# ACT work that waits for DVE moved behind the next product's PSUM copy; transposes and routing spread over more slots

## The chip, the cores and the metric

The kernel runs on one core of a Trainium2 chip as one launch. A core has TensorE (PE) for matrix products, VectorE (DVE), ScalarE (ACT) and GpSimd (POOL) for elementwise work, SyncE (SP) that issues DMAs, an on-chip memory (SBUF) and the accumulators (PSUM) that PE writes. Each engine runs its own instructions strictly in the order in which the program emits them, and waits on semaphores for the others. The metric is device time in microseconds, from several runs of the same program; the profile shows one further execution.

## The reference

```
attn = softmax(q @ mean_pool8(k).T / sqrt(64)) @ mean_pool8(v)    # 4 batches, 8 heads, 576 rows, 64 wide
x = attn as [2304, 512]
P = exp(x @ w_gate - max);  8 times: P /= row sums; P /= column sums; P *= N / E     # routing, [2304, 8]
x = sum over 8 experts e of P[:, e] * (relu(x @ w1[e]) @ w2[e])   # 512 -> 1024 -> 512
g = x @ gate;  out = (g * sigmoid(g) * (x @ val)) @ out_w         # 512 -> 1536 -> 512, float64 weights
```

## The kernel before

Every product is made in three float32r passes: an operand is split into a high part (ACT copies it, `hh`, `ph`, `r`) and a low part (POOL or DVE subtracts the high part from the source, `hl`, `pl`), and PE multiplies high by high, high by low and low by high (lines 114 to 116 for the first layers, 1002 to 1004 for the second). A first phase computes attention and the first half of expert 0; there the eight routing rounds begin. The rest is 90 *quads* of expert work (three passes over 768 tokens, 30 quads each) and then 36 quads of the gated layer (18 steps of a gate quad and a value quad).

A quad computes a 2 by 2 block product by Winograd's seven products M1, M2, M5, M6, M7, M4, M3 in this order (`quad`). M1 goes to the PSUM tile `a`, M2 to `b`, M5 to `c`; M6, M7 and M4 accumulate on `a`, M3 on `c`. Partial sums are taken by ACT copies out of PSUM (line 948): `s1` after M1, `u2` after M6, `u3` after M7. So M6, which adds to `a` again, must wait for the copy `s1`, and M7 for `u2`. The four results 11, 22, 21, 12 go through a *sink*: DVE adds the partial sum (`csum`, line 1017), ACT takes the ReLU as high part (`hh`, 1019), DVE takes the low part (`hl`, 1020). 21 needs no sum and is read from PSUM directly. The second-layer tiles of the quad before (`ys`, six per quad, three PSUM buffers) are put in two at a time by `fill_y` after M6, M7 and M4; DVE adds each to its accumulator (`acc`, line 1107).

The order is written out by hand. After each product, and after each second-layer tile, `pump` runs what stands in `late` (DVE low parts, sigmoids), then the tasks that `next_weights` and the pass boundaries put at that product (splits of the next weights, `pair_hi` on ACT and `pair_lo` on POOL; splits of the token operands B11, B21, B22, T1 to T4; loads), then one step of the queue `side`. A quad has 13 such side slots when it has six tiles. `side` holds the routing (`route_rows`, one slot of nothing, `route_cols`), the transposes of finished tokens at the start of a pass (`transposed`: PE transposes into a `y` buffer, ACT copies it to `x2`, which has two buffers, SP stores it), and in passes 2 and 3 the conversion of the float64 weights (`convs`: DVE integer steps `c64t`, `c64s`, `c64u`, a POOL addition `c64w` and POOL sums).

In `quad` the sink is called before `pump`: ACT's `hh` of result 12, which waits for DVE's `csum`, is emitted after M3 and so stands in ACT's queue ahead of the next quad's `s1` copy, and `hl` is emitted right behind it.

Of the kernel before, what the change touches and what calls it, by code (L numbers as in the profile page):

```python
# [28 lines left out]
def fused_kernel(ctx: ExitStack, tc, q, k, v, w_gate, w1, w2, v_gate, v_val, v_out, out):  # L29
# [472 lines left out]
    with tc.manual_schedule():  # L502
# [146 lines left out]
        def load_pair(i):  # L649
            if i < len(quads):  # L650
                praw[i] = rawp.tile([P, KD, 2 * P], F32, tag="raw", name=f"praw{i}")
                if i < NE:
                    nc.sync.dma_start(out=praw[i], in_=quads[i].rearrange("(k p) f -> p k f", p=P))
                else:
                    n, g = quads[i]
                    nc.sync.dma_start(out=praw[i].rearrange("p k f -> p (k f)"), in_=w32_d[n][:, g])

        def row_of(i):
# [122 lines left out]
        for _ in range(ITERS):  # L781
            side.extend([route_rows, nothing, route_cols])

# [167 lines left out]
        def pump(tasks, m):  # L951
            later()
            for t in tasks.get(m, ()):
                t()
            if side:
                side.popleft()()

        def quad(i, ys, tasks, sink):

            def fill_y(n):  # L960
                for _ in range(n):
                    if ys:
                        ys.popleft()()
                        pump({}, None)

            per = -(-len(ys) // 3)
# [3 lines left out]
            pump(tasks, "M1")  # L970
# [6 lines left out]
            pump(tasks, "M5")  # L977
            product(a, i, "M6", False)
            u2 = part_sum(a, "u2")
            pump(tasks, "M6")  # L980
            fill_y(per)
            product(a, i, "M7", False)
            u3 = part_sum(a, "u3")
            sink("22", c, u3)
            pump(tasks, "M7")
            fill_y(per)
            product(a, i, "M4", False)
            sink("21", a, None)
            pump(tasks, "M4")
# [79 lines left out]
        for n in range(NS):  # L1069
# [3 lines left out]
            if l == 3:  # L1073
                merge(tasks, {m: [lambda t=t: scale_first(t), lambda t=t: scale_first(t + 1)]
                              for m, t in zip(("M1", "M2", "M5"), range(p * TT, (p + 1) * TT, 2))})
            if l == 4:
# [9 lines left out]
            if l == 1 and p > 0:  # L1086
                side.extendleft(reversed([lambda t=t: transposed(t) for t in range((p - 1) * TT, p * TT)]))
            if n == 3:
                assert not side
            if p > 0 and l not in (0, 1, SP1 - 1):  # L1090
                while len(side) < 13:
                    step = next(convs, None)
                    if step is None:
                        break
                    side.append(step)
            if n == 2:
                ahead["w"].close()
# [20 lines left out]
        gp = ctx.enter_context(tc.tile_pool(name="gp", bufs=1, **left))  # L1118

        nc.scalar.activation(out=small[:, 3:4], in_=ones[:, 0:1], func=AF.Sigmoid)  # L1120

        def gate_sink(gs):
            def sink(name, ps, t):
# [10 lines left out]

                late.append(sigmoid)
                gs[name] = g
# [21 lines left out]
        for m in range(NS2):  # L1158
# [65 lines left out]
```

## Time and profile before

| | us |
|---|---|
| median of 3 runs | 2152.66 (2148.53 to 2158.32) |
| profiled execution | 2159.88 |
| its span, first to last instruction | 2158.2 |
| PE busy / DVE / ACT / POOL | 2078.4 / 1495.3 / 826.6 / 1179.2 |
| mean granted TensorE clock | 0.986 |

The span is what the profiler recorded of the program; the 1.7 us between it and the time lie around it. Busy time is the time in which an engine had an instruction running; for PE it includes time at a lower granted clock (1.0 is 2.4 GHz, 0.5 is 1.2 GHz). The rows that the prediction reads stand below, after the change.

### The profile page before, as it was taken

The numbers are of one execution on the slowest core, as the hardware profiler recorded it, in microseconds if no ns is written. First come the engines' busy times: TensorE is split into PE (matmuls) and PEld (weight loads), VectorE is DVE, ScalarE is ACT, GpSimd is POOL, SyncE is SP. The second block draws the span as 40 slices with busy tenths as digits, with TensorE's granted clock in tenths as the row PEclk, the third lists the DMA queues.
The fourth block names the chain that finished last, engine by engine and source line by source line (L and its number), as shares of the span: only waits on it lengthen the run. The fifth ranks groups of instructions, "written<-read, shape, count | busy, mean of one in ns | idle before, by whom it ended". The sixth has DMA issues, their size and how long they took to land.

```text
span 2158.2 us, 28175 instructions
## 1 busy us (share of the span) xinstructions
PE 2078.4 (96%) x10622; PEld 1868.6 (87%) x10622; DVE 1495.3 (69%) x2271; ACT 826.6 (38%) x1587; POOL 1179.2 (55%) x1088
## 2 busy tenths in 40 slices
PE   8989899999999999999999999999999999999999
PEld 7878798999899888888988888888888888898898
DVE  7664756555555588878888678888878746656565
ACT  3433343443434432333333422333323454444543
POOL 4444466565656556666566556666566444434332
PEclk9999999999999999999999999999999999999999
DMA  6343344343444444443434434444334454543432
GB/s 178 100 99 74 107 147 156 117 148 126 144 130 136 138 137 156 156 145 128 137 127 156 132 107 162 138 156 147 117 129 141 145 194 143 173 161 126 147 137 98
DMA packets 153048, 296.49 MB, mean 137 GB/s; under 512 B 28240, under 2 KB 107088, under 8 KB 139088
## 3 DMA queue, kind: packets, MB, share of 16 engines
q1 hardware_dynamic: 139376, 216.05, 30.9%
q0 software_dynamic: 13536, 78.65, 11.3%
q8 instruction: 83, 1.36, 0.3%
q14 instruction: 53, 0.43, 0.1%
HBM read 223.89 MB, written 70.78 MB: 137 GB/s over the span
## 4 chain that ended last, share of the span: by engine, by line
PE 72%; DVE 20%; ACT 4%; issue 2%; DMA 1%; POOL 1%; ACTq 0%; SPq 0%; DVEq 0%; POOLq 0%
PE yps L1003 11%; PE yps L1002 11%; PE yps L1004 11%; PE aps L114 7%; PE aps L115 7%; PE aps L116 7%; DVE acc L1107 3%; PE cps L116 3%; PE cps L115 3%; PE cps L114 3%; DVE hl L1020 2%; DVE csum L1017 1%; PE bps L114 1%; PE bps L115 1%; PE bps L116 1%
## 5 line engine op out<-in xcount | busy, mean ns | idle before, releaser
L1002 PE MATMUL yps<-r,hh 128*128 128x512 f32 x1296 | 512.1, 395 | 10.0 <-DVE acc L1107 8.9
L1003 PE MATMUL yps<-r,hh 128*128 128x512 f32 x1296 | 513.1, 396 | 0.0
L1004 PE MATMUL yps<-r,hl 128*128 128x512 f32 x1296 | 511.3, 395 | 0.0
L1107 DVE SCALAR_TENSOR_TENSOR acc<-yps,pr,acc 128x512 f32<-128x512 f32 x504 | 365.1, 744 | 117.0 <-PE yps L1004 116.8
L715 POOL TENSOR_TENSOR pl<-sums,ph 128x1024 fp32r<-128x1024 f32 x125 | 303.7, 2429 | 236.0 <-ACT ph L709 236.0
L715 POOL TENSOR_TENSOR pl<-praw,ph 128x512 fp32r<-128x512 f32 x250 | 270.5, 1103 | 264.2 <-ACT ph L709 249.9
L1019 ACT ACTIVATE hh<-csum 128x384 fp32r<-128x384 f32 x270 | 141.9, 526 | 609.4 <-DVE csum L1017 609.4
L1002 PEld LDWEIGHTS yps<-r,hh 128*128 128x128 f32 x1296 | 245.9, 190 | 54.8 <-DVE acc L1107 13.2
L1004 PEld LDWEIGHTS yps<-r,hl 128*128 128x128 f32 x1296 | 245.8, 190 | 53.8
L1020 DVE SCALAR_TENSOR_TENSOR hl<-csum,hh 128x384 fp32r<-128x384 f32 x270 | 170.5, 631 | 158.6 <-ACT hh L1019 158.6
L1003 PEld LDWEIGHTS yps<-r,hh 128*128 128x128 f32 x1296 | 245.8, 190 | 38.8
L948 ACT COPY u<-aps 128x384 f32<-128x384 f32 x252 | 120.3, 478 | 275.7 <-PE aps L116 274.3
L66 POOL TENSOR_TENSOR r<-rraw,r 128x512 fp32r<-128x512 f32 x72 | 96.4, 1342 | 181.8 <-ACT r L65 181.2
L1017 DVE TENSOR_TENSOR csum<-cps,u 128x384 f32<-128x384 f32 x180 | 99.5, 553 | 60.1 <-ACT u L948 46.3
L709 ACT ACTIVATE ph<-sums 128x1024 fp32r<-128x1024 f32 x125 | 130.8, 1046 | 1.6 <-POOL sums L688 1.6
L709 ACT ACTIVATE ph<-praw 128x512 fp32r<-128x512 f32 x250 | 117.5, 521 | 0.0
L114 PE MATMUL aps<-T2h,ph 128*128 128x384 f32 x250 | 89.8, 359 | 27.8 <-ACT s L948 26.8
L1185 DVE TENSOR_TENSOR o<-yps,o 128x512 f32<-128x512 f32 x90 | 62.0, 689 | 55.4 <-PE yps L1004 55.4
L115 PE MATMUL aps<-T2l,ph 128*128 128x384 f32 x250 | 86.5, 346 | 1.0 <-DVE T2l L602 1.0
L888 POOL TENSOR_TENSOR c64w<-c64s,c64u 128x512 f32<-128x512 f32 x36 | 47.2, 1311 | 72.8 <-DVE c64u L882 68.3
L114 PE MATMUL aps<-T3h,ph 128*128 128x384 f32 x250 | 85.9, 344 | 0.6 <-ACT u L948 0.6
L116 PE MATMUL aps<-T2h,pl 128*128 128x384 f32 x250 | 86.0, 344 | 0.0
(258 smaller groups left out, 4808.2 us busy)
## 6 DMA issues: line engine op xcount, KB each, us to landing
r<-rows_d POOLq DMA_DIRECT2D x72, 1024.0 KB, 5.4
praw<-in_moe_w_dram SPq DMA_DIRECT2D x90, 512.0 KB, 4.7
rows_d<-r SPq DMA_DIRECT2D x36, 1024.0 KB, 6.3
rraw<-in_moe_w_dram SPq DMA_DIRECT2D x30, 512.0 KB, 4.2
praw<-gate_d SPq DMA_DIRECT2D x18, 512.0 KB, 7.1
sums<-gates_d SPq DMA_DIRECT2D x18, 512.0 KB, 3.9
praw<-val_d SPq DMA_DIRECT2D x18, 512.0 KB, 4.6
sums<-vals_d SPq DMA_DIRECT2D x18, 512.0 KB, 3.8
```

What stands on the lines that cost most here:

```text
L114: nc.tensor.matmul(ps, lhsT=wh, rhs=ah, start=start, stop=False, skip_group_check=more)
L115: nc.tensor.matmul(ps, lhsT=wh, rhs=al, start=False, stop=False, skip_group_check=more)
L116: nc.tensor.matmul(ps, lhsT=wl, rhs=ah, start=False, stop=stop, skip_group_check=more)
L709: nc.scalar.activation(out=hi, in_=src, func=AF.Copy)
L715: nc.gpsimd.tensor_tensor(out=lo, in0=src, in1=hi.bitcast(F32), op=ALU.subtract)
L1002: nc.tensor.matmul(ps, lhsT=hh[:, o:o + P], rhs=wh, start=j == 0, stop=False)
L1003: nc.tensor.matmul(ps, lhsT=hh[:, o:o + P], rhs=wl, start=False, stop=False)
L1004: nc.tensor.matmul(ps, lhsT=hl[:, o:o + P], rhs=wh, start=False, stop=j == 1)
L1017: nc.vector.tensor_tensor(out=src, in0=ps[:, :HB], in1=t, op=ALU.add)
L1019: nc.scalar.activation(out=hh, in_=src, func=AF.Relu)
L1020: late.append(lambda: nc.vector.scalar_tensor_tensor(out=hl, in0=src, scalar=0.0, in1=hh.bitcast(F32), op0=ALU.max, op1=ALU.subtract))
L1107: nc.vector.scalar_tensor_tensor(out=acc[t], in0=ps, scalar=pr[:, t, e:e + 1], in1=acc[t], op0=ALU.mult, op1=ALU.add)
```

## The change

`pump` no longer runs `late`. A new helper `after(m, ...)` in `quad` runs `late` first, then the sinks, then `pump`; `fill_y` runs `late` itself. In the expert sink, the pair of ACT's `hh` and DVE's `hl` is no longer emitted at once where a sum is taken (11, 22, 12) but put on `late`, so that `hh` is emitted one product later and `hl` another one; 21, which ACT reads from PSUM, is emitted at once. The gate sink's sigmoid of 21 is emitted at once too.

```diff
         def pump(tasks, m):
-            later()
             for t in tasks.get(m, ()):
                 t()
             if side:
...
+            def after(m, *steps):
+                later()
+                for name, ps, t in steps:
+                    sink(name, ps, t)
+                pump(tasks, m)
...
             product(b, i, "M2", True)
-            sink("11", b, s1)
-            pump(tasks, "M2")
+            after("M2", ("11", b, s1))
...
             product(c, i, "M3", False)
-            sink("12", c, u2)
-            pump(tasks, "M3")
+            after("M3", ("12", c, u2))
...
-                nc.scalar.activation(out=hh, in_=src, func=AF.Relu)
-                late.append(lambda: nc.vector.scalar_tensor_tensor(
-                    out=hl, in0=src, scalar=0.0, in1=hh.bitcast(F32), op0=ALU.max, op1=ALU.subtract))
+                def parts():
+                    nc.scalar.activation(out=hh, in_=src, func=AF.Relu)
+                    late.append(lambda: nc.vector.scalar_tensor_tensor(
+                        out=hl, in0=src, scalar=0.0, in1=hh.bitcast(F32), op0=ALU.max, op1=ALU.subtract))
+                if t is None:
+                    parts()
+                else:
+                    late.append(parts)
```

On ACT, at the boundary of the same two expert quads in pass 2: before, the two `hh` of 21 and 12, then the copy `s`, then `hh` of 11 and the copy `u` (u2).

```order
637 L709 ACTIVATE ph<-sums 128x1024
638 L1019 ACTIVATE hh<-aps 128x384
639 L1019 ACTIVATE hh<-csum 128x384
640 L948 COPY s_8389<-aps 128x384
641 L1019 ACTIVATE hh<-csum 128x384
642 L948 COPY u_8427<-aps 128x384
```

After (line numbers of the new file: 1088 is `hh`, 1012 the copy, 773 the high part of the next weights):

```order
598 L773 ACTIVATE ph<-sums 128x1024
599 L1088 ACTIVATE hh<-csum 128x384
600 L1088 ACTIVATE hh<-aps 128x384
601 L1012 COPY s_8437<-aps 128x384
602 L1088 ACTIVATE hh<-csum 128x384 x2
603 L1012 COPY u_8476<-aps 128x384
```

The copy `s` has moved ahead of `hh` of 12, which now stands with `hh` of 11 between `s` and `u`; `hh` of 22 has moved behind `ph<-sums`.

On DVE, the same quad boundary before: `csum` and `hl` of 12, `csum` and `hl` of 11, then a conversion step and the accumulations.

```order
856 L1017 TENSOR_TENSOR csum<-cps,u_8275 128x384
857 L1020 SCALAR_TENSOR_TENSOR hl<-csum,hh 128x384
858 L1017 TENSOR_TENSOR csum<-bps,s_8389 128x384
859 L1020 SCALAR_TENSOR_TENSOR hl<-csum,hh 128x384
860 L861 TENSOR_SCALAR c64t<-c64t 128x512
```

After (1084 is `csum`, 1089 `hl`, 916 and 919 a conversion step):

```order
882 L1084 TENSOR_TENSOR csum<-cps,u_8322 128x384
883 L1089 SCALAR_TENSOR_TENSOR hl<-csum,hh 128x384
884 L1084 TENSOR_TENSOR csum<-bps,s_8437 128x384
885 L916 TENSOR_SCALAR c64t<-craw 128x512
886 L919 TENSOR_SCALAR c64t<-c64t 128x512
887 L1089 SCALAR_TENSOR_TENSOR hl<-csum,hh 128x384
```

A conversion step stands now between `csum` and `hl` of 11; `hl` of 12 still stands directly behind its `csum` where the side slot after M1 is empty.

The diff also adds a `pair_lo` that makes the subtraction of the 1024-wide sums in two halves of 512. It stands in front of a second copy of the functions from `row_of` to `pair_hi`, and behind that copy the old `pair_lo` is still defined, so the later definition is the one that the tasks call:

```diff
         def pair_lo(i, what):
...
+                    n = 2 if j == 2 else 1
+                    if j in what:
+                        for c in range(n):
+                            part = (slice(None), slice(c * src.shape[1] // n, (c + 1) * src.shape[1] // n))
+                            nc.gpsimd.tensor_tensor(out=lo[part], in0=src[part], in1=hi[part].bitcast(F32),
+                                                    op=ALU.subtract)
+
+        def row_of(i):
...
+        def pair_lo(i, what):
+            if i < len(quads):
+                for j, (src, hi, lo) in enumerate(pair_views(i)):
                     if j in what:
                         nc.gpsimd.tensor_tensor(out=lo, in0=src, in1=hi.bitcast(F32), op=ALU.subtract)
```

On POOL, one expert quad in pass 1, before:

```order
293 L688 TENSOR_TENSOR sums<-praw_5349,sums 128x256
294 L715 TENSOR_TENSOR pl<-praw_5349,ph 128x512
295 L715 TENSOR_TENSOR pl<-praw_5349,ph 128x256
296 L715 TENSOR_TENSOR pl<-sums,ph 128x1024
297 L66 TENSOR_TENSOR r<-rraw_5406,r 128x512 x2
```

After:

```order
293 L752 TENSOR_TENSOR sums<-praw_5348,sums 128x256
294 L779 TENSOR_TENSOR pl<-praw_5348,ph 128x512
295 L779 TENSOR_TENSOR pl<-praw_5348,ph 128x256
296 L779 TENSOR_TENSOR pl<-sums,ph 128x1024
297 L66 TENSOR_TENSOR r<-rraw_5404,r 128x512 x2
```

Nothing moved there: POOL still makes the subtraction of the sums as one instruction of 1024 elements.

The rest of the change is in the side queue and the tasks:

```diff
-        LAST = {"M2": operands("B11"), "M6": operands("B21"), "M7": operands("T1"), "M3": operands("T2")}
-        FIRST = {"M1": operands("T3"), "M2": operands("T4"), "M6": operands("B22")}
+        LAST = {"M2": operands("B11"), "M6": operands("B21"), "M7": operands("T1"), "M4": operands("T2")}
+        FIRST = {"M1": operands("T3"), "M5": operands("T4"), "M7": operands("B22")}
...
-            side.extend([route_rows, nothing, route_cols])
+            side.extend([route_rows, nothing, nothing, route_cols, nothing])
...
             if l == 1 and p > 0:
-                side.extendleft(reversed([lambda t=t: transposed(t) for t in range((p - 1) * TT, p * TT)]))
+                for t in range((p - 1) * TT, p * TT):
+                    side.extend([lambda t=t: transposed(t), nothing, nothing, nothing])
...
-            if p > 0 and l not in (0, 1, SP1 - 1):
+            if n >= SP1 - 6 and l not in (0, 1, SP1 - 1):
                 while len(side) < 13:
...
             if m == 1:
-                side.extend([lambda t=t: transposed(t) for t in range((NPASS - 1) * TT, NPASS * TT)])
+                for t in range((NPASS - 1) * TT, NPASS * TT):
+                    side.extend([lambda t=t: transposed(t), nothing, nothing, nothing, nothing])
```

Six scalings of accumulators in quad 3 are spread over five products instead of three, and the table load for the sigmoid stands after M4 of the last expert quad instead of behind it.

## Rows read from the trace of the kernel before

**Rows 1.** Windows by stage: length, busy PE, PEld, DVE, ACT, POOL, clock, DMA

```profile
205.00:256.00 51.00, 39.99 (x220) 34.95 (x219) 37.74 (x93) 20.30 (x39) 21.47 (x16) 0.93 0.25 83
256.00:700.00 444.00, 444.00 (x2211) 401.92 (x2211) 249.47 (x382) 181.39 (x344) 282.43 (x256) 1.00 0.42 138
700.00:1690.00 990.00, 962.73 (x4734) 860.78 (x4733) 784.98 (x1140) 326.91 (x627) 598.84 (x565) 0.99 0.43 141
1690.00:2154.00 464.00, 447.96 (x2255) 408.63 (x2254) 291.58 (x456) 218.85 (x419) 182.99 (x131) 0.98 0.43 145
```

**Rows 2.** Waits of PE over the whole run: us in total, times, longest

```profile
PE aps L114 <- ACT s L948: 26.8, 21, 3.3
PE yps L1002 <- DVE acc L1107: 8.9, 8, 2.3
...
PE mps L769 <- DVE cs L764: 6.3, 4, 2.5
PE sps L769 <- DVE cs L764: 4.2, 2, 2.5
PE sps L1051 <- ACT x L1053: 3.9, 3, 2.9
...
PE yps L1002 <- ACT x L1053: 1.0, 1, 1.0
```

**Rows 3.** Windows behind two waits: columns as in rows 1, the clock third from last

```profile
1278.00:1282.00 4.00, 4.00 (x13) 3.23 (x13) 1.97 (x4) 1.69 (x4) 1.97 (x2) 0.57 0.27 79
1329.00:1337.00 8.00, 6.71 (x19) 5.72 (x20) 3.33 (x7) 2.73 (x6) 1.96 (x2) 0.57 0.23 66
```

**Rows 4.** Timeline of PE in one quad: starts of M1, M2, first tile, M7

```profile
1291.38 0.34 PE L114 MATMUL aps<-B11h,ph 128*128 128x384 f32 x1
...
1292.44 0.34 PE L114 MATMUL bps<-B21h,ph 128*128 128x384 f32 x1
...
1295.62 0.40 PE L1002 MATMUL yps<-r,hh 128*128 128x512 f32 x1
...
1298.36 0.34 PE L114 MATMUL aps<-T3h,ph 128*128 128x384 f32 x1
```

**Rows 5.** Timeline of DVE, ACT and PE around the longest wait for the copy

```profile
1328.78 0.54 DVE L1017 TENSOR_TENSOR csum<-cps,u 128x384 f32<-128x384 f32 x1
1329.90 0.56 DVE L1020 SCALAR_TENSOR_TENSOR hl<-csum,hh 128x384 fp32r<-128x384 f32 x1 [0.59 <-ACT hh L1019]
...
1329.78 0.46 ACT L948 COPY s<-aps 128x384 f32<-128x384 f32 x1
1330.97 0.52 ACT L1019 ACTIVATE hh<-csum 128x384 fp32r<-128x384 f32 x1 [0.73 <-DVE csum L1017]
...
1330.29 0.69 PE L114 MATMUL aps<-T2h,ph 128*128 128x384 f32 x1 [3.33 <-ACT s L948]
```

**Rows 6.** Timeline of DVE, ACT and PE at a pass boundary of the gated layer

```profile
1998.65 2.52 DVE L602 TENSOR_TENSOR T1l<-xq,T1h 128x768 fp32r<-128x768 f32 x1 [1.13 <-ACT T1h L601]
...
2005.17 0.96 DVE L602 TENSOR_TENSOR T2l<-xq,T2h 128x768 fp32r<-128x768 f32 x1 [0.18 <-ACT T2h L601]
...
2003.88 0.52 ACT L1150 ACTIVATE hh<-g 128x384 fp32r<-128x384 f32 x1 [1.69 <-DVE g L1146]
2005.40 0.84 ACT L601 ACTIVATE T3h<-xq 128x768 fp32r<-128x768 f32 x1
...
2005.55 0.69 PE L114 MATMUL aps<-T2h,ph 128*128 128x384 f32 x1 [3.18 <-ACT s L948]
```

**Rows 7.** Timeline of ACT at the transposes of the gated layer

```profile
1735.17 0.58 ACT L1053 COPY x<-sps 128x512 f32<-128x512 f32 x1 [2.86 <-DMA x_d<-x]
```

**Rows 8.** Timeline of POOL and DVE ahead of the longest wait for an accumulation

```profile
1004.79 2.55 POOL L715 TENSOR_TENSOR pl<-sums,ph 128x1024 fp32r<-128x1024 f32 x1
...
1005.03 2.59 DVE L863 TENSOR_SCALAR c64s<-craw 128x512 uint32<-128x512 uint32 x1
```

**Rows 9.** Group of DVE by line and form, 760 to 1690 us: count, busy, mean, idle

```profile
L1020 DVE SCALAR_TENSOR_TENSOR hl<-csum,hh 128x384 fp32r<-128x384 f32 x170 | 106.9, 629 | 100.0 <-ACT hh L1019 100.0
```

More of the change, by code (lines that the diff above doesn't have):

```diff
@@ L656, in load_pair, with load_rows @@
                     nc.sync.dma_start(out=praw[i].rearrange("p k f -> p (k f)"), in_=w32_d[n][:, g])
+        def row_of(i):
+            if i < NE:
+                p, l = divmod(i, NE // NPASS)
+                return l, p
+            p, l = divmod(i - NE, NG)
+            return NE // NPASS + l, p
+        def load_rows(i):
+            if i < len(rows) and row_of(i)[1] == 0:
+                rraw[i] = rawp.tile([P, 2, DM], F32, tag="raw", name=f"rraw{i}")
+                if i < NE:
+                    nc.sync.dma_start(out=rraw[i], in_=rows[i].rearrange("(j p) d -> p j d", p=P))
+                else:
+                    n, g = rows[i]
+                    nc.sync.dma_start(out=rraw[i].rearrange("p j d -> p (j d)"), in_=w32_d[n][:, g])
@@ new lines, in load_sums, with take_sums @@
+        def load_sums(i):
+            if NE <= i < len(quads):
+                n, g = quads[i]
+                sums[i] = sp.tile([P, 4, 2, P], F32, tag="sums", name="sums")
+                nc.sync.dma_start(out=sums[i].rearrange("p a k f -> p (a k f)"), in_=sums_d[n][:, g])
+        def take_sums(r, t):
+            a11, a12, a21, a22 = (r[:, k:k + 2, c:c + P] for c in (0, P) for k in (0, 2))
+            G = nc.gpsimd
+            G.tensor_tensor(out=t[:, 0], in0=a21, in1=a22, op=ALU.add)
+            G.tensor_tensor(out=t[:, 1], in0=t[:, 0], in1=a11, op=ALU.subtract)
+            G.tensor_tensor(out=t[:, 2], in0=a11, in1=a21, op=ALU.subtract)
+            G.tensor_tensor(out=t[:, 3], in0=a12, in1=t[:, 1], op=ALU.subtract)
@@ new lines, in pair_sums, with pair_views @@
+        def pair_sums(i):
+            if i < NE:
+                sums[i] = sp.tile([P, 4, 2, P], F32, tag="sums", name="sums")
+                take_sums(praw[i], sums[i])
+        def pair_views(i):
+            wh, wl = psets[i]
+            r = praw[i]
+            yield r[:, :, 0:P], *(w[:, 0:4] for w in (wh, wl))
+            yield r[:, 2:4, P:2 * P], *(w[:, 4:6] for w in (wh, wl))
+            yield sums[i].rearrange("p a k f -> p (a k f)"), *(w[:, 6:14].rearrange("p a f -> p (a f)") for w in (wh, wl))
@@ new lines, in pair_hi @@
+        def pair_hi(i, what):
+            if i < len(quads):
+                if i not in psets:
+                    psets[i] = [wp.tile([P, 14, P], F32R, tag=f"p{h}", name=f"p{h}") for h in "hl"]
+                for j, (src, hi, lo) in enumerate(pair_views(i)):
+                    if j in what:
+                        nc.scalar.activation(out=hi, in_=src, func=AF.Copy)
+        def pair_lo(i, what):
+            if i < len(quads):
+                for j, (src, hi, lo) in enumerate(pair_views(i)):
+                    n = 2 if j == 2 else 1
+                    if j in what:
+                        for c in range(n):
+                            part = (slice(None), slice(c * src.shape[1] // n, (c + 1) * src.shape[1] // n))
+                            nc.gpsimd.tensor_tensor(out=lo[part], in0=src[part], in1=hi[part].bitcast(F32),
+                                                    op=ALU.subtract)
@@ L963, in fill_y @@
                         ys.popleft()()
+                        later()
                         pump({}, None)
+            def after(m, *steps):
+                later()
+                for name, ps, t in steps:
+                    sink(name, ps, t)
+                pump(tasks, m)
             per = -(-len(ys) // 3)
@@ L969, in quad @@
             s1 = part_sum(a, "s1")
-            pump(tasks, "M1")
+            after("M1")
             b = ps_b.tile([P, 512], F32, tag="b", name="bps")
             product(b, i, "M2", True)
-            sink("11", b, s1)
-            pump(tasks, "M2")
+            after("M2", ("11", b, s1))
             c = ps_c.tile([P, 512], F32, tag="c", name="cps")
             product(c, i, "M5", True)
-            pump(tasks, "M5")
+            after("M5")
             product(a, i, "M6", False)
             u2 = part_sum(a, "u2")
-            pump(tasks, "M6")
+            after("M6")
             fill_y(per)
@@ L1073, in fused_kernel @@
             if l == 3:
-                merge(tasks, {m: [lambda t=t: scale_first(t), lambda t=t: scale_first(t + 1)]
-                              for m, t in zip(("M1", "M2", "M5"), range(p * TT, (p + 1) * TT, 2))})
+                merge(tasks, {m: [lambda t=p * TT + t: scale_first(t)]
+                              for t, m in enumerate(("M1", "M2", "M5", "M6"))})
+                merge(tasks, {"M7": [lambda t=p * TT + t: scale_first(t) for t in (4, 5)]})
             if l == 4:
@@ L1095, in fused_kernel @@
                     side.append(step)
+            if n == NS - 1:
+                merge(tasks, {"M4": [lambda: nc.scalar.activation(out=small[:, 3:4], in_=ones[:, 0:1], func=AF.Sigmoid)]})
             if n == 2:
@@ L1133, in sigmoid @@
                     late.append(lambda: nc.vector.tensor_tensor(out=g, in0=src, in1=sg, op=ALU.mult))
-                late.append(sigmoid)
+                if t is None:
+                    sigmoid()
+                else:
+                    late.append(sigmoid)
                 gs[name] = g
```

8 lines of the change are left out of this document (3 added, 5 removed).

## The prediction

> **What bounds the kernel now.** I read the busy time by stage first [rows 1]. PE is the bound everywhere from 205 us on: it is busy 444 of 444 us in pass 0, 962.7 of 990 us in passes 1 and 2, 448 of 464 us in the gated layer. No PE work is removed, so all that can be won is its idle time and the time that it ran at a lower clock. Idle is 11.0 us in the routing stretch (51 less 40.0), 0 in pass 0, 27.3 us in passes 1 and 2 and 16.0 us in the gated layer: 54.3 us. The list of PE's waits [rows 2] names nearly all of it: 26.8 us for the copy `s1` in 21 waits, 8.9 us for DVE's accumulation to free a second-layer buffer, 10.5 us (6.3 and 4.2) for the routing sums, 4.9 us (3.9 and 1.0) for the transposes' copies.
>
> Then the clock. Behind a long wait the granted clock falls to 0.5 (1.2 GHz) for some microseconds: four microseconds at a mean of 0.57 behind a wait of 2.5 us, eight at 0.57 behind one of 3.3 us [rows 3]. At 0.57, four microseconds hold 1.7 us less work and eight hold 3.4. Ten such stretches stand behind 205 us in windows of 1 us: two after routing waits (1.7 each), two after transposes (1.7 each), one after an accumulation wait (1.7) and five after waits for `s1` (three of 1.7 and two of 3.4, 11.9 in all). With the waits that led to them:
>
> - `s1`: 26.8 + 11.9 = 38.7 us
> - routing: 10.5 + 3.4 = 13.9 us
> - accumulation: 8.9 + 1.7 = 10.6 us
> - transposes: 4.9 + 3.4 = 8.3 us
>
> That is 71.5 us of the 2159.9 us of the profiled execution. If all went and nothing came, the time would be 2088.4 us, the floor.
>
> **The s1 waits, 28 of 38.7 us won.** PE's own pace: a product takes 1.06 us, two second-layer tiles 2.74 us [rows 4]. From the end of M3, M6 starts 3.2 us later (M1, M2, M5). Before, `s1` stands behind `hh` of 12, which waits for DVE's `csum` of 12: with 0.52 us for `hh` and 0.46 for the copy, `csum` may end some 2.1 us after M3. At the longest wait DVE did nothing but work through its queue and began that `csum` at 1328.78, when M5 had ended; PE stood 3.33 us [rows 5]. Now `s1` waits for PE alone, and M6 never for DVE. What is late next is `u2`, for which M7 waits: it stands behind both `hh` of 12 and of 11. Its need comes 3.8 us after that of `s1` (M6 and two tiles), but DVE must first do `hl` of 12, which waits for `hh` (0.59 us and 0.56), and `csum` of 11, and ACT `hh` of 11 (0.52): in rows 5 `hh` of 11 begins at 1330.97, 1.6 to 1.7 us behind `hh` of 12. So the new order bears about 2.1 us more lateness, and a wait w leaves w - 2.1: of 3.33 us 1.2, of 2.51 us 0.4, of all waits under 2.1 nothing.
>
> At the two pass boundaries of the gated layer it is worse. PE stood 3.18 us in one [rows 6] and as long in the other. There `hh` of 12 comes at 2003.88; the new order has T3's high part (0.84) behind it, then DVE T3's low part (0.96 like T2's) ahead of the sum of 11, then the sum (0.54), ACT the sigmoid (taken at 0.52 like `hh`), T4's high part (0.84, now after M5) and only then `u2`, which ends at about 2008.5. PE could have begun M6 at 2002.37 (3.18 before 2005.55), so it wants M7 3.8 us later at 2006.2: 2.3 us. T2's split, which stood ahead of `s1`, is moved ahead of M3 and costs nothing there. With 1 us for the other boundaries the remains are 1.2 + 0.4 + 4.6 + 1 = 7.2 us, and 3.4 us of lower clock behind two of them: 28 us are won. Bounds: 38.7 (DVE's queue gets shorter too), 10 (DVE gets later).
>
> **Transposes, 8 of 8.3 us.** PE waits for a `y` buffer, this for ACT's copy to `x2`, this for the store of the tile before the last (2.86 us idle behind the DMA) [rows 7]. Six transposes stood in neighbouring slots; now three or four empty slots lie between, at least three products or 3.2 us each time, so the store ends beside PE's work. The same 18 transposes, copies and stores are issued. Bounds 4 to 8.3.
>
> **Routing, 9.4 of 13.9 us.** Each round's column product waits for DVE's chain of row steps; one product or unit more lies between now, and one more behind. PE's order shows the first column product where it was, so its wait (10.5 us in six, so some 1.75) stays; five of the eight rounds now lie in the first two quads, beside the splits of T4 and B22, the sums of those quads and POOL's work, where waits of 2.5 us occurred [rows 2]. I keep twice the 1.75 us of wait and 1 us of clock. Bounds 4 to 13.9.
>
> **Accumulation, 4.5 of 10.6 us.** DVE sits behind `hh` for 100 us between 760 and 1690 us before `hl` [rows 9]. With `hl` one slot behind `hh` most of this goes for 22, 21 and 11. For 12 it can grow: `hl` stands directly behind its `csum`, and `hh` now waits for M1 and `s1`; this gives back about half. What made the longest wait of PE [rows 2] was something else: a conversion step of DVE took 2.59 us while POOL's 1024-wide subtraction ran for 2.55 us [rows 8]. T1's low part likewise took 2.52 us where T2's, of the same shape, took 0.96 [rows 6]. The halves would shorten this, but the order shows POOL's instruction unchanged, since the old `pair_lo` is defined again behind the new one. So the blocking stays, and I count half of the waits. Bounds 0 to 10.6.
>
> The Trainium skill, "SBUF — State Buffer", section "SBUF: two separate sides", says that DVE and GpSimd share a port pair as an exclusive lock, and whoever starts first holds it for the whole instruction. The trace agrees (2.59 us beside 2.55 us [rows 8]). By it, halves in force would cut the longest block to half and this term would be nearly all won, 6 us more; with the order as it is, the rule leaves the term where I put it.
>
> **New costs, 5 us.** Conversion steps start in the last quads of pass 0, where PE had no idle and DVE was busy 249 of 444 us [rows 1]; those quads also split and store rows. At the idle rate of passes 1 and 2 (27.3 of 990 us, some 0.4 us a quad) five quads cost 2 us. B22 and T4 come later but before the products that read them (M3, M4). Conversion loads now stand on SP's queue between the row stores and weight loads of pass 0. I add 3 us for this and for `hl` of 12. Bounds 0 to 12.
>
> **Sum.** 28 + 8 + 9.4 + 4.5 - 5 = 44.9 us, say 45: 2159.9 - 45 = 2114.9 in the profiled execution's own terms. The median of the runs shown is 7.2 us lower. PE's work being the same in each run, that spread should lie in the waits, most of which go, so I take two thirds of the 7.2 off, 5 us: 2110 us. The likeliest case's own range is 2094 to 2126.
>
> **Rivals.**
>
> - DVE's pace decides. In passes 1 and 2 it is busy 785 of 990 us [rows 1]; if `hl` of 12 makes it stand until M1, `s1` and `hh` are through in each of some 57 conversion quads, it stays late, half of the `s1` gain turns into waits for `u2` and the accumulation gains nothing. Then 14 + 8 + 9.4 - 5 = 26 us are won: with the same 5 us off, about 2129 us. For it: no spare side slot there. Against: the mean leaves a fifth of DVE's time free. Chance 0.15.
> - The waits only change their name: M7 waits for `u2` as long as M6 did for `s1`. Only transposes and routing are won, less the new cost, 12.4 us: about 2142 us, on the edge of no change. Against: the need comes 3.8 us later [rows 4]. Chance 0.08.
> - Slower: `u2`, behind two `hh` that each wait for DVE, is late in every quad, not only where DVE lags. If M7 stood 1 us in each of the 126 quads, that is 126 us against the 56 us of the other terms (38.7 + 8 + 9.4): 2160 + 126 - 56 - 5 = 2225 us. It decides from 0.45 us per quad on. Against: `s1`, with less room, was late in 21 of 126 quads [rows 2]. Chance 0.05.
> - The halves don't do what the diff says; this is in the forecast. Were they in force: 6 us less, about 2104 us.
>
> **How the numbers follow.** The forecast has 0.72. Half a per cent, some 11 us, is what a measurement of this kernel can tell. The forecast and the first rival end below 2141.9; the second splits around it; so faster 0.86, same 0.08, slower 0.06. The range of 8 in 10 goes from 2090 (just over the floor, all waits gone) to 2132 (the first rival).
>
> **What would show it.** Right: PE's waits for `s` nearly gone from the list, a small wait for `u` in their place, 2 us at two boundaries of the gated layer; DVE's idle time before `hl` less by half; no waits for `x`; POOL's subtraction of 1024 elements still there as one instruction; fewer windows at clock 0.5. Wrong: waits for `u` over 15 us, waits for the accumulation over 9 us, PE idle in pass 0, or a median above 2132 us.

## The result, and the profile after

The changed kernel takes 2100.05 us in the median of 4 runs (2099.61 to 2101.5); the kernel before 2152.85 us in four. The ratio is 0.9755, with an interval of 0.9732 to 0.9777: 52.8 us faster. The forecast was 2110 us, in a range of 2090 to 2132, so the gain was 10 us larger than forecast. The profiled execution's span fell by 60.3 us, from 2158.2 to 2097.9 us; 5 us of this are low clock ahead of 180 us (10.2 us lost before, 5.1 after, in windows of 1 us), where the change moves nothing.

Windows by stage of the changed kernel, columns as in [rows 1]; the stages end a little earlier, since the program is shorter:

```profile
205.00:256.00 51.00, 45.75 (x247) 39.55 (x246) 41.29 (x85) 24.19 (x45) 29.87 (x24) 0.97 0.33 114
256.00:698.00 442.00, 440.02 (x2189) 397.67 (x2189) 303.33 (x421) 174.49 (x340) 294.48 (x259) 1.00 0.44 143
698.00:1651.00 953.00, 949.92 (x4738) 856.97 (x4738) 768.61 (x1113) 324.68 (x629) 592.60 (x554) 1.00 0.43 143
1651.00:2094.00 443.00, 431.47 (x2227) 399.07 (x2225) 314.70 (x450) 215.82 (x412) 179.57 (x129) 1.00 0.44 150
```

PE's idle time in the four stages is 5.3, 2.0, 3.1 and 11.5 us, 21.8 in all, against 54.3 us [rows 1]. Passes 1 and 2 gave 24.2 us of it, and their clock is at full level throughout. The gated layer gave 4.5 us, and 6.8 us of low clock.

The stages got shorter by more than that. From the first product of pass 1 to that of the gated layer it was 989.3 us and is 951.0, 38.3 us less, of which 24.2 are idle time and 8.5 low clock; from there to the end it was 460.8 us and is 445.9, 14.9 less, of which 4.5 and 6.8. The other 9.2 us (5.6 and 3.6) stood as busy time of PE beside the waits. Four quads of the kernel before, each from its M1 to the next M1, columns as in [rows 1]:

```profile
1584.73:1602.41 17.68, 15.96 (x79) 14.13 (x79) 13.67 (x23) 5.18 (x10) 9.86 (x9) 1.00 0.46 149
1602.41:1618.08 15.67, 15.67 (x79) 14.19 (x79) 12.41 (x20) 5.21 (x10) 8.04 (x7) 1.00 0.24 71
1879.91:1891.83 11.92, 11.84 (x62) 10.73 (x62) 5.66 (x9) 6.72 (x13) 5.43 (x5) 1.00 0.65 229
1891.83:1903.39 11.56, 11.56 (x62) 10.79 (x62) 5.52 (x10) 6.64 (x13) 3.85 (x4) 1.00 0.28 92
```

The first pair are expert quads, one with a wait of 1.72 us and one with none: the wait made the quad 2.01 us longer, 0.29 us more than itself. The second pair are a gate quad and its value quad: the idle time is only 0.08 us, too short for the list of waits [rows 2], and the quad is 0.36 us longer. In the kernel before 22 quads of passes 1 and 2 have a wait at full clock, and nearly all of them take 0.28 to 0.36 us more than the wait; in the gated layer 12 gate quads have the short one. In the changed kernel 6 such quads are left in passes 1 and 2, and the short ones are gone.

What PE waited for, columns as in [rows 2]; the lines between are of the attention phase:

```profile
PE aps L114 <- ACT u L1012: 11.8, 8, 2.8
...
PE cps L116 <- POOL pl L779: 2.5, 2, 1.7
PE mps L833 <- DVE cs L828: 2.1, 2, 1.5
PE yps L1069 <- DVE acc L1186: 2.1, 4, 1.0
...
PE cps L115 <- DVE B22l L602: 1.7, 2, 0.9
...
PE sps L833 <- DVE cs L828: 0.9, 1, 0.9
```

The waits for `s` (26.8 us) and for `x` (4.9 us) are gone without a rest. Waits for accumulations fell from 8.9 to 2.1 us, for the routing sums from 10.5 to 3.0 us. New are 11.8 us for `u` (1.2 us before), and some for POOL's low parts of the weights and for B22.

The two longest waits for `u` are where the forecast put them, at the pass boundaries of the gated layer. Timeline of ACT, DVE and PE at the first of the two:

```profile
1799.39 0.46 ACT L1012 COPY s<-aps 128x384 f32<-128x384 f32 x1
1801.96 0.53 ACT L1229 ACTIVATE hh<-g 128x384 fp32r<-128x384 f32 x1 [2.10 <-DVE g L1225]
1802.39 0.83 ACT L601 ACTIVATE T3h<-xq 128x768 fp32r<-128x768 f32 x1
1804.71 0.52 ACT L1208 ACTIVATE sg<-g 128x384 f32<-128x384 f32 x1 [1.49 <-DVE g L1203]
1805.14 0.83 ACT L601 ACTIVATE T4h<-x 128x768 fp32r<-128x768 f32 x1
1805.87 0.46 ACT L1012 COPY u<-aps 128x384 f32<-128x384 f32 x1
...
1803.25 0.96 DVE L602 TENSOR_TENSOR T3l<-xq,T3h 128x768 fp32r<-128x768 f32 x1 [0.18 <-ACT T3h L601]
1804.13 0.55 DVE L1203 TENSOR_TENSOR g<-bps,s 128x384 f32<-128x384 f32 x1
...
1800.95 0.34 PE L114 MATMUL aps<-T2h,ph 128*128 128x384 f32 x1
...
1806.38 0.44 PE L114 MATMUL aps<-T3h,ph 128*128 128x384 f32 x1 [2.83 <-ACT u L1012]
```

The copy `s` is now done 2.1 us before `hh` of 12 is begun. From there the chain runs as in the working: `hh`, T3's high part, DVE's low part of T3, the sum of 11, the sigmoid, T4's high part, `u`. M6 begins at 1800.95; M7 (with T3) stood 2.83 us, and 2.84 at the other boundary.

DVE's `hl` behind `csum`, first in the kernel before, and POOL's subtraction of the sums, over the whole run (count, busy us, mean ns, idle before):

```profile
L1020 DVE SCALAR_TENSOR_TENSOR hl<-csum,hh 128x384 fp32r<-128x384 f32 x270 | 170.5, 631 | 158.6 <-ACT hh L1019 158.6
...
L1089 DVE SCALAR_TENSOR_TENSOR hl<-csum,hh 128x384 fp32r<-128x384 f32 x270 | 237.2, 879 | 104.0 <-ACT hh L1088 103.9
...
L779 POOL TENSOR_TENSOR pl<-sums,ph 128x1024 fp32r<-128x1024 f32 x125 | 305.7, 2446 | 105.0 <-ACT ph L773 104.3
```

POOL's subtraction is one instruction of 1024 elements still. DVE's idle time before `hl` fell only from 158.6 to 104.0 us, by a third and not by half as forecast, and one `hl` takes longer (0.88 us against 0.63). With POOL's subtraction in halves it takes 0.80 (b1_halves), so part of that comes from POOL.

### The profile page after: what moved, and what is told of

It is laid out like the page before. It is cut to its first block, busy times and chain, and to the rows that moved or that the text cites. A ratio compares the mean times of both kernels' runs of the same rounds, so it can differ in the third digit from the quotient of the medians.

```text
span 2097.9 us, 28075 instructions
## 1 busy us (share of the span) xinstructions
PE 2050.0 (98%) x10622; PEld 1854.9 (88%) x10622; DVE 1558.2 (74%) x2271; ACT 819.2 (39%) x1587; POOL 1192.2 (57%) x1088
## 4 chain that ended last, share of the span: by engine, by line
PE 87%; DVE 8%; POOL 2%; ACT 2%; issue 1%; DMA 1%; ACTq 0%; POOLq 0%; DVEq 0%
PE yps L1069 13%; PE yps L1070 13%; PE yps L1071 13%; PE aps L114 8%; PE aps L116 8%; PE aps L115 8%; PE cps L116 4%; PE cps L115 4%; PE cps L114 4%; PE bps L114 2%; PE bps L115 2%; PE bps L116 2%; PE mps L270 1%; PE hps L114 1%; PE yps L126 1%
## 5 line engine op out<-in xcount | busy, mean ns | idle before, releaser
L1186 DVE SCALAR_TENSOR_TENSOR acc<-yps,pr,acc 128x512 f32<-128x512 f32 x504 | 373.5, 746 | 132.5 <-PE yps L1071 129.3
L779 POOL TENSOR_TENSOR pl<-praw,ph 128x512 fp32r<-128x512 f32 x250 | 264.4, 1078 | 281.0 <-ACT ph L773 269.8
L779 POOL TENSOR_TENSOR pl<-sums,ph 128x1024 fp32r<-128x1024 f32 x125 | 305.7, 2446 | 105.0 <-ACT ph L773 104.3
L1089 DVE SCALAR_TENSOR_TENSOR hl<-csum,hh 128x384 fp32r<-128x384 f32 x270 | 237.2, 879 | 104.0 <-ACT hh L1088 103.9
L1012 ACT COPY s<-aps 128x384 f32<-128x384 f32 x126 | 60.4, 480 | 449.0 <-PE aps L116 449.0
L66 POOL TENSOR_TENSOR r<-rraw,r 128x512 fp32r<-128x512 f32 x72 | 103.4, 1457 | 179.1 <-ACT r L65 174.8
L787 POOL DMA_DIRECT2D r<-rows_d x72 | 42.5, 591 | 111.0 <-PE yps L1071 108.3
L1088 ACT ACTIVATE hh<-aps 128x384 fp32r<-128x384 f32 x90 | 44.2, 492 | 144.0 <-PE aps L116 143.9
L116 PE MATMUL cps<-T1h,pl 128*128 128x384 f32 x250 | 85.1, 340 | 2.5 <-POOL pl L779 2.5
```

Source lines behind the costliest of these rows:

```text
L116: nc.tensor.matmul(ps, lhsT=wl, rhs=ah, start=False, stop=stop, skip_group_check=more)
L779: nc.gpsimd.tensor_tensor(out=lo, in0=src, in1=hi.bitcast(F32), op=ALU.subtract)
L1012: nc.scalar.copy(out=t, in_=ps[:, :HB])
L1089: late.append(lambda: nc.vector.scalar_tensor_tensor(out=hl, in0=src, scalar=0.0, in1=hh.bitcast(F32), op0=ALU.max, op1=ALU.subtract))
L1186: nc.vector.scalar_tensor_tensor(out=acc[t], in0=ps, scalar=pr[:, t, e:e + 1], in1=acc[t], op0=ALU.mult, op1=ALU.add)
```

## The experiments

Times are medians against the kernel before on the same chip.

### The new order alone (a1_order)

The kernel before with the edits to `pump`, `quad` and the sinks, and nothing else of the change.

```diff
-            sink("12", c, u2)
-            pump(tasks, "M3")
+            after("M3", ("12", c, u2))
```

> The kernel before with the new order alone (sinks behind what is late, hh and hl put off); transposes, routing, conversions and token splits as before. Theory (the copy s1 stood behind hh of 12): PE's waits for s fall from 26.8 us to under 2, the low clock behind them goes, time 2153 - 30 = about 2123 us, with some 7 us of waits for u instead. Rival (the gain comes from what was spread in the side queue and the earlier conversions, and the waits only change their name): waits for u about as long as those for s were, time about 2148 us.

Measured: 2103.39 us (2099.3 to 2105.89) against 2152.09, ratio 0.9775 (0.976 to 0.979): 48.7 us. Waits of PE:

```profile
PE mps L769 <- DVE cs L764: 6.2, 4, 2.5
PE aps L114 <- ACT u L948: 4.7, 7, 1.4
PE sps L769 <- DVE cs L764: 4.3, 2, 3.0
PE sps L1061 <- ACT x L1063: 2.8, 1, 2.8
...
PE yps L1005 <- DVE acc L1117: 2.4, 5, 0.8
```

No wait for `s` is left, `u` took over 4.7 us, and the accumulations fell to 2.4 us. The theory held, and the gain was larger than its 30 us: by the table of the prediction, all of the `s1` term (38.7 us) and 6.5 of the 8.9 us of accumulation waits with the 1.7 us of clock behind them, less 3.5 us more for `u` (4.7 for 1.2): 43 us. The other 5 us are about what the waits cost beyond their own length: PE's busy time, less the low clock, is 6 us shorter than in the kernel before. At the two pass boundaries of the gated layer M7 waits only 0.27 us for `u` here, behind a wait of 0.80 us for T2's low part at M6. The order alone makes nearly the whole result, as the splits of the change stand; b3_oldsplits below shows what they hide.

### Everything but the order (a2_rest)

```diff
-            side.extend([route_rows, nothing, route_cols])
+            side.extend([route_rows, nothing, nothing, route_cols, nothing])
...
-        FIRST = {"M1": operands("T3"), "M2": operands("T4"), "M6": operands("B22")}
+        FIRST = {"M1": operands("T3"), "M5": operands("T4"), "M7": operands("B22")}
...
-            if p > 0 and l not in (0, 1, SP1 - 1):
+            if n >= SP1 - 6 and l not in (0, 1, SP1 - 1):
```

(with the transposes, scalings and table load of the change)

> Everything of the change but the new order: transposes and routing over more slots, conversions from the end of pass 0, token splits, scalings and the table load moved. Theory: waits for s stay near 27 us, those for x and half of those for the routing go, time about 2153 - 17 + 3 = 2139 us; together with the order alone this adds up to the whole gain of 53 us within 8 us. Rival: waits for s fall below 10 us too, because DVE is relieved, time about 2115 us.

Measured: 2150.1 us, ratio 0.9989 (0.9979 to 0.9998): 2 us, where 13 were expected.

```profile
PE aps L114 <- ACT s L948: 23.0, 21, 3.6
PE yps L1002 <- DVE acc L1112: 13.0, 9, 3.1
...
PE cps L115 <- DVE B22l L602: 6.1, 3, 2.1
PE sps L769 <- DVE cs L764: 4.8, 3, 2.5
```

Routing and transposes did shorten their waits, but B22, split later, came late three times (6.1 us), accumulations cost 13.0 instead of 8.9 us, and PE stood in pass 0, where it had not (435.94 us busy of 444 between 256 and 700 us, 2.9 of the idle us in the first 24). The rival fell too: waits for `s` stayed. With the order alone the sum is 50.7 of the 52.8 us.

### Transposes alone (a3_trans), routing alone (a4_route)

```diff
-                side.extendleft(reversed([lambda t=t: transposed(t) for t in range((p - 1) * TT, p * TT)]))
+                for t in range((p - 1) * TT, p * TT):
+                    side.extend([lambda t=t: transposed(t), nothing, nothing, nothing])
```

> The kernel before with the transposes alone spread over more slots. Theory: the 4.9 us of waits for x and the 3.4 us of low clock behind them go, time about 2145 us. Rival (the y buffers and ACT's copies now collide with the second-layer tiles in later slots): under 3 us won, 2150 us or more.

Measured: 2147.33 us, ratio 0.9981 (0.997 to 0.9991), 4.8 us won; no wait for `x` is left. The waits go as expected, the time by 4.8 of 8 us.

The routing kernel has only the longer list of empty slots.

> The kernel before with the routing rounds alone spread over more slots. Theory: 9 of 14 us go, the first column product still waits, time about 2144 us. Rival (the rounds only move into the first quads, where DVE is full): waits in the first three quads grow by as much, time 2150 us or more.

Measured: 2149.3 us, ratio 0.999 (0.9976 to 1.0004), 2.8 us, no clear gain. Windows of this kernel, columns as in [rows 1]:

```profile
205.00:256.00 51.00, 45.01 (x256) 39.17 (x255) 39.63 (x83) 23.52 (x46) 28.71 (x24) 1.00 0.35 114
256.00:280.00 24.00, 21.31 (x99) 18.72 (x98) 18.11 (x36) 7.37 (x14) 12.15 (x10) 0.93 0.32 111
```

In the routing stretch 5.0 us of idle time and the low clock went [rows 1], but the rounds now reach into the 24 us behind it, where PE was never idle before and is now 2.7 us, with the clock at 0.93. So the rival was partly right. In the changed kernel the same 24 us are almost free of it: 0.2 us idle between 250 and 280 us, in windows of 1 us.

### Only hl put off (c1_hl), only hh of 12 put off (c2_hh12)

These take the new order apart, in the expert quads.

```diff
-                late.append(lambda: nc.vector.scalar_tensor_tensor(
-                    out=hl, in0=src, scalar=0.0, in1=hh.bitcast(F32), op0=ALU.max, op1=ALU.subtract))
+                late.append(lambda: late.append(lambda: nc.vector.scalar_tensor_tensor(
+                    out=hl, in0=src, scalar=0.0, in1=hh.bitcast(F32), op0=ALU.max, op1=ALU.subtract)))
```

> The kernel before with one thing put off: DVE's hl of the expert quads is emitted one slot later, ACT's hh and its place ahead of s1 as before. Theory A (ACT's order made the s1 waits): DVE's idle time before hl falls from 159 us to under 90, but waits for s stay above 15 us, time about 2135 us. Theory B (DVE, standing behind hh, was what made csum and so s1 late): waits for s under 8 us, time about 2115 us.

Measured: 2152.59 us, ratio 1.0 (0.999 to 1.0009).

```profile
PE aps L114 <- ACT s L948: 30.0, 15, 3.3
...
PE yps L1002 <- DVE acc L1107: 2.1, 2, 1.5
...
L1020 DVE SCALAR_TENSOR_TENSOR hl<-csum,hh 128x384 fp32r<-128x384 f32 x270 | 182.0, 674 | 87.1 <-ACT hh L1019 87.0
```

DVE stood 87 instead of 159 us behind `hh`, and PE's waits for accumulations fell from 8.9 to 2.1 us, yet the time is the same: fewer but longer waits for `s`, 30.0 us. Relieving DVE without moving `s1` is worth nothing. Theory B falls; A was right on the waits and 17 us too hopeful on the time.

```diff
+                def parts():
...
+                if name == "12":
+                    late.append(lambda: late.append(parts))
+                else:
+                    parts()
```

> The kernel before with one thing put off: hh of result 12 alone, which goes behind the next quad's copy s1 (and its hl with it), in the expert quads; the gated layer as before. Theory A: waits for s fall to the 11 us of the gated layer, time about 2125 us, as near to the order alone as the gated layer lets it. Theory B: waits for s turn into waits for u of 10 us or more, DVE stays late, time 2140 us.

Measured: 2129.81 us, ratio 0.9884 (0.9864 to 0.9904): 23 us from moving one ACT instruction per expert quad, and its `hl` behind it.

```profile
PE aps L114 <- ACT s L948: 9.9, 4, 3.2
PE yps L1002 <- DVE acc L1112: 8.2, 8, 2.4
```

The four waits left for `s` are those of the gated layer, which this kernel leaves as it was. The accumulation waits stay at 8.2 us. So the two waits have two causes: `s` waited because of ACT's order, the accumulations because the `hl` of the other results held DVE behind `hh`.

### The halves in force (b1_halves)

```diff
-                    if j in what:
-                        nc.gpsimd.tensor_tensor(out=lo, in0=src, in1=hi.bitcast(F32), op=ALU.subtract)
+                    n = 2 if j == 2 else 1
+                    if j in what:
+                        for c in range(n):
+                            part = (slice(None), slice(c * src.shape[1] // n, (c + 1) * src.shape[1] // n))
+                            nc.gpsimd.tensor_tensor(out=lo[part], in0=src[part], in1=hi[part].bitcast(F32),
+                                                    op=ALU.subtract)
```

The later definition of `pair_lo` gets the halves.

> The changed kernel with the halves in force: POOL subtracts the sums as 2 x 512 in place of 1 x 1024. Theory (POOL's long subtraction blocks DVE, but with the new order DVE has slack): DVE's mean hl on csum falls from 0.88 us towards 0.7, waits of PE for accumulations fall from 2.1 us under 1, time 2100 - 1 to 3 us = about 2098. Rival (the two shorter instructions end later, since DVE gets in between): waits of PE for pl grow from 2.8 us to over 6, time 2104 or more.

Measured: 2093.89 us (2091.62 to 2095.56) against 2150.81, ratio 0.973 (0.9709 to 0.975). The changed kernel, measured at another time, had 2100.05, and b2_convlate below, measured at the same time, 2100.65: 6 us less, the number that the prediction had for halves in force.

```profile
PE yps L1073 <- DVE acc L1190: 0.9, 1, 0.9
PE aps L116 <- POOL pl L782: 0.4, 1, 0.4
...
L602 DVE TENSOR_TENSOR T1l<-xq,T1h 128x768 fp32r<-128x768 f32 x6 | 7.7, 1279 | 1.8 <-ACT T1h L601 1.6
...
L782 POOL TENSOR_TENSOR pl<-sums,ph 128x512 fp32r<-128x512 f32 x250 | 355.9, 1444 | 108.5 <-ACT ph L773 108.3
```

T1's low part in the kernel before, then B22's and T1's in the changed one:

```profile
L602 DVE TENSOR_TENSOR T1l<-xq,T1h 128x768 fp32r<-128x768 f32 x6 | 14.2, 2373 | 3.2 <-ACT T1h L601 3.2
```

```profile
L602 DVE TENSOR_TENSOR B22l<-x,B22h 128x768 fp32r<-128x768 f32 x6 | 12.7, 2124 | 0.6 <-ACT B22h L601 0.2
...
L602 DVE TENSOR_TENSOR T1l<-xq,T1h 128x768 fp32r<-128x768 f32 x6 | 12.1, 2018 | 1.8 <-ACT T1h L601 1.6
```

POOL spends 50 us more (355.9 against 305.7 us for the same subtraction), off the path. T1's low part falls from a mean of 2.02 us in the changed kernel to 1.28. Waits for POOL's low parts shrink from 2.8 to 0.4 us instead of growing; why they shrink was not tried (the first half ends earlier). The rival falls, and the gain is larger than the 1 to 3 us of the theory. Of it 1.2 us are waits for accumulations; 2.4 are waits for POOL's low parts, 1.7 for B22 and 1.8 for `u`, against 1.2 more for the routing sums.

### Conversions late again (b2_convlate)

```diff
-            if n >= SP1 - 6 and l not in (0, 1, SP1 - 1):
+            if p > 0 and l not in (0, 1, SP1 - 1):
```

> The changed kernel with conversions only from pass 1 on, as before. Theory (they cost some waits in pass 0, 2 idle us between 256 and 700, and buy little behind it): time about 2098 to 2100 us. Rival (the earlier start is what leaves DVE slack in passes 1 and 2): waits for u and for accumulations grow by over 8 us, time about 2110.

Measured: 2100.65 us (2098.63 to 2102.58), ratio 0.9762 (0.9741 to 0.9782), the same as the changed kernel. Pass 0 is free of idle time again, and waits for `u` rise from 11.8 to 16.0 us. The earlier start of the conversions is worth nothing that can be measured.

### The token splits at other products (b3_oldsplits, b4_bound)

First the old places, in the changed kernel:

```diff
-        LAST = {"M2": operands("B11"), "M6": operands("B21"), "M7": operands("T1"), "M4": operands("T2")}
-        FIRST = {"M1": operands("T3"), "M5": operands("T4"), "M7": operands("B22")}
+        LAST = {"M2": operands("B11"), "M6": operands("B21"), "M7": operands("T1"), "M3": operands("T2")}
+        FIRST = {"M1": operands("T3"), "M2": operands("T4"), "M6": operands("B22")}
```

> The changed kernel with the token splits at their old products (T2 at M3, T4 at M2, B22 at M6). Theory: T2's low part is late for M6 again (1 to 2 us), u2 at the boundaries is no later than in the changed kernel; waits for B22 (1.7 us) go; time 2100 to 2103. Rival (the move of the splits was needed for the new order): waits of PE at the five pass boundaries grow from some 13 us to over 20, time 2110.

Measured: 2090.54 us (2089.53 to 2090.97), ratio 0.9713 (0.9691 to 0.9736): some 10 us less than the changed kernel (9 by the ratios). Both expectations missed: the move of the splits does harm. Then a place behind the copy `u2`:

```diff
-        FIRST = {"M1": operands("T3"), "M5": operands("T4"), "M7": operands("B22")}
+        FIRST = {"M2": operands("T3"), "M6": operands("T4", "B22")}
```

> The changed kernel with T3 split at M2 instead of M1 and T4 and B22 at M6, behind the copy u2 (T2 stays at M4). Theory (at the boundaries u2 stands behind T3, T4 and the chain of 11, 2.3 us late at each in the gated layer): waits of PE for u fall from 11.8 us to under 5, the low clock behind the longest goes, time about 2100 - 8 = 2092. Rival (DVE, not ACT's order, is late there): waits for u stay above 9 us or turn into waits for T3, T4 or B22, time 2098 to 2102.

Measured: 2089.31 us (2089.01 to 2092.42), ratio 0.9712 (0.9692 to 0.9732). Waits of PE, first with the old places, then behind `u2`:

```profile
PE aps L114 <- ACT u L1012: 5.5, 8, 1.4
...
PE aps L115 <- DVE T2l L602: 1.6, 2, 0.8
```

```profile
PE aps L114 <- ACT u L1012: 5.9, 6, 1.4
...
PE cps L116 <- POOL pl L779: 2.5, 2, 1.7
```

In both, the waits for `u` halve to under 6 us, their longest from 2.8 to 1.4 us, and the 1.7 us for B22 are gone; the 1.7 us of low clock behind the boundary too. Waits and clock make 9 us of the 10 to 11. So the moved splits hid what the rest of the change gives beside the new order: b3_oldsplits, which is a1_order with the transposes, the routing, the conversions, the scalings and the table load, is 12.9 us below it (13 by the ratios), where transposes and routing alone gave 4.8 and 2.8.

### Both together (c3_best, c4_best2)

Halves in force, with the splits of b4_bound; and with T3, T4 and B22 at their old products, T2 at its new one.

> The changed kernel with two edits together: halves in force, and T3 split at M2, T4 and B22 at M6. The two gained 6 and 11 us alone, at different places (POOL's blocking of DVE within the passes; the pass boundaries): if they add, 2083 us; if the boundaries' waits came from POOL's blocking too, 2087 or more.

Measured: 2087.21 us (2086.59 to 2088.22) against 2152.83, ratio 0.9691 (0.9677 to 0.9706), the fastest median of all, 12.8 us below the changed kernel.

> The changed kernel with the halves in force and T3, T4 and B22 split at their old products (M1, M2, M6), T2 at its new one (M4). Theory: the two gains of 6 and 10 us add, 2084 us, within 3 us of the version with the splits put off further; rival: T4 at M2, ahead of hh of 11, costs 1.5 us at each boundary once POOL's blocking is shorter, 2090 us.

Measured: 2090.68 us (2086.72 to 2092.39), ratio 0.9706 (0.9688 to 0.9723). In its trace the rival's cost is there: at each of the two boundaries M7 waits 2.10 us for `u`, and 0.97 in c3_best.

Waits of PE for `u`, first in c3_best, then in c4_best2:

```profile
PE aps L114 <- ACT u L1016: 4.9, 7, 1.0
```

```profile
PE aps L114 <- ACT u L1016: 8.1, 9, 2.1
```

The boundaries show what the place of each split costs. In the first quad behind a pass boundary of the gated layer, M7 begins 8.61 us behind M1 in the changed kernel and in b1_halves, 7.88 in c4_best2 (T4 at M2 again), 7.10 in b3_oldsplits (T2 at M3 again as well) and 6.75 in b4_bound. So T4's place costs 0.73 us and T2's 0.78, at each of the two boundaries. At M5 T4's high part stands on ACT behind the sigmoid of 11, which waits for DVE, and ahead of `u2`; at M2 ACT does it while it would stand. At M4 T2's low part stands on DVE ahead of the sum of 12.

Whether the gains of halves and splits add is not shown. By the times they don't: halves gave 6 us to the changed kernel and 2 to b4_bound, and c3_best misses the 2083 us of the addition by 4. By the ratios to the kernel before, each taken at its own time, they do: 0.9755 less 0.0025 and 0.0043 is 0.9687, and 0.9691 was measured. In c3_best the accumulation wait is 0.9 us and the waits for `u` are 4.9 us, as the addition would have it, and between 280 and 1690 us PE is idle 1.3 us against 3.9 us in b4_bound. But its profile has 11.9 us lost at low clock ahead of 180 us, b4_bound 6.8 us, in code that is the same. The clock differs from run to run of one kernel: the four runs of c4_best2 have a mean granted clock of 0.993 to 0.997, and the one at 0.997 is the shortest (2086.72 us), one at 0.993 the longest (2092.39). The runs of c3_best have 0.993 to 0.995, three of the four of b4_bound 0.997; by an estimate from these, 0.0025 of 2087 us, that is some 5 us, as much as c3_best lacks. A few microseconds between two kernels can come from there.

## Why the prediction was right

- **PE is the bound, and its waits and low clock are what can be won.** Right, but not all of it: a wait also lengthened the quad by some 0.3 us beyond its own idle time, which no list of waits shows. The 71.5 us came from the list of waits and the windows of low clock; the fastest version, 2087.2 us, came out at the floor of 2088.4 us with 10 us of waits behind 205 us still in its list. That floor was in the profiled execution's terms, 7 us above the median, and left out these 0.3 us and the low clock of the first phase.
- **`s1`, 28 of 38.7 us.** Right in mechanism; the size is right in part by luck. The `s` waits and the 11.9 us of low clock behind them went; 11.8 us of `u` waits and 1.7 us of clock came, net 25 us, or 26 with the 1.2 us of `u` before. But the pieces are others than those worked out. Within the passes of the expert quads no wait for `u` is left, where 1.6 us were to stay. In the gated layer I took the pace of an expert quad, M7 3.8 us behind M6; there two second-layer tiles take 1.4 us instead of 2.74, and M7 could begin 2.6 us behind M6 (1800.95, and 1806.38 less 2.83). So two waits of 1.76 us for `s`, of which nothing was to stay, left 1.40 us for `u` each, and by the right pace the boundaries' 2.3 us would have been 3.5. That 2.83 were measured is due to `hh` of 12, which begins 1.0 us behind the start of M6 and not 1.5 us behind the moment at which M6 could have started.
- **The splits at the boundaries.** Wrong in two places, both inside the `s1` term. I said that T2's split, moved ahead of M3, costs nothing: on DVE its low part now stands ahead of the sum of 12, for 0.78 us. And I booked T4's high part ahead of `u2` under the new order: 0.73 us of it come from T4's new product. With the order alone (a1_order) a boundary costs 0.80 and 0.27 us, not 2.83.
- **Accumulation, 4.5 of 10.6 us.** Mis-sized. 6.8 us of waits and 1.7 us of low clock went, 8.5. I gave POOL's lock half of the term; c1_hl shows that `hl` standing behind `hh` made most of it. POOL's blocking made part of the rest: 2.1 us fell to 0.9 with the halves in force. The 6 us that I gave to halves in force were measured, but by luck: the accumulation had 1.2 of them, and the others came from POOL's low parts, B22 and `u`. The rule of the Trainium skill ("SBUF — State Buffer", section "SBUF: two separate sides": the port pair is held for the whole instruction) agrees with the traces: in the changed kernel the four low parts of T1 that began while POOL's 1024-wide subtraction ran took 2.54 to 2.57 us and ended 0.8 us behind its end, and one that began 0.05 us ahead of it took 0.96. With the halves in force the four took 1.42 to 1.46.
- **Transposes, 8 us.** Right in the trace (4.9 us of waits and the low clock gone), 4.8 us when timed alone. With routing 17.4 us were forecast; beside the new order, with the splits at their old products, the rest of the change gave 12.9.
- **Routing, 9.4 us.** 7.5 us of waits and 1.7 us of clock went in the changed kernel, but alone it gave 2.8 us, not clear of zero, since the rounds brought waits into the next quads. In the changed kernel the quads behind are nearly free of them: 0.2 us of idle time between 250 and 280 us. The new order made the room there: a2_rest, which lacks only the order, has 3.7 us in the same window.
- **New costs, 5 us.** Right in size: 2.0 us in pass 0, 1.7 us for B22, 2.8 us for POOL's low parts (2.5 and 0.3; 1.7 of it is in pass 0 and so counted twice here). One step failed: I said that the later split of B22 comes before the product that reads it. B22 came late twice; moved to M7, its low part ran beside POOL's subtraction and took 2.12 us on the mean. In the kernel before it took 1.01 us, and with the halves in force 1.37, with no wait.
- **Why 53 and not 43 us.** In the profiled executions 44.9 us were forecast and 60.3 measured. Of the 15 us between them 9 are what the waits cost beyond their length, 5 the low clock ahead of 180 us, which the forecast did not have, and 4 the accumulation; some 3 us went the other way. Then I took 5 us off for the median, since the spread of the runs should lie in waits that go. The changed kernel's median is 0.4 us above its profiled execution, so this step failed; it brought the number nearer by luck. The spread of the kernel before goes with the clock: in 25 further runs from 2147.38 us at a mean of 0.992 to 2158.84 us at 0.986, which is also that of the profiled execution.
- **Rivals.** DVE's pace did not decide, though `hl` of 12 does stand behind `s` as feared (104 us of idle time left): DVE had that time. The waits did not merely change their name (a1_order: 26.8 us became 4.7). `u` was late 8 times, in 7 quads, not in every one.

## What to carry to other kernels

On an in-order engine look at what stands in the queue between the moment at which the bounding engine could go on and the copy that lets it: one instruction that waits for a third engine, ahead of a copy that waits for nobody else, cost 23 us here and was cured by its place alone. Freeing the third engine from its own idle time, with the order left as it was, gave nothing. When work is put off, follow it to the next thing that the bounding engine waits for, and list all that now stands ahead of it, the rare steps at stage boundaries too; and look in the order whether an edit is in force at all.

## What the runs showed of the hardware

A shorter instruction on POOL freed DVE although POOL's own busy time grew by 50 us: T1's low part, of one shape throughout, had a mean of 2.37 us before, 2.02 us with the new order and 1.28 us with the halves. A wait of PE cost more than its idle time: at full clock most expert quads with a wait took 0.28 to 0.36 us more than the 15.67 us of one without and the wait together, and an idle time of 0.08 us made a gate quad 0.36 us longer (11.92 against 11.56 us). The low clock ahead of 180 us, in code that no version changed, cost between 5.1 and 11.9 us in the profiles.
